# Two halves of the first layer's weights fetched and converted ahead of the first attention units

## The chip, the cores and the metric

The kernel runs on one core of one Trainium2 chip. Times are device microseconds of one execution; the time before is the median of three runs. Besides the times there is one profiled execution, whose trace all rows below come from.

## What is computed

A block of local and global attention, and behind it two feed-forward layers, all in float32. 4 batches with 8 heads, 512 local and 32 global positions of 64 values each; the attention's rows, 2176 of 512 values, go through the two layers, each 512 to 2048 to 512.

```python
s_g = scale * np.matmul(q_g, k_all.transpose(0, 1, 3, 2))
out_g = np.matmul(sm(s_g), v_all)
mask = np.abs(pos[:, None] - pos[None, :]) <= window
s_ll = np.where(mask, s_ll, -1000000000.0)
s_l = np.concatenate([s_lg, s_ll], axis=-1)
out_l = np.matmul(sm(s_l), np.concatenate([v_g, v_l], axis=2))
...
h = x @ w_in                                       # first layer
g = np.maximum(h, 0.0) + alpha * np.minimum(h, 0.0)
x = g @ w_out
h = x @ w_in2                                      # second layer
g = h * np.clip(h + 3.0, 0.0, 6.0) / 6.0
out = g @ w_out2
```

## The kernel before

**Units.** Local attention is cut into 32 units, each a batch, one of two halves of the sequence and a pair of heads. A unit loads queries and keys (`qk_t`, 368 KB, L169) and values (`v_t`, 512 KB, L180). `scores` (L187 and on) takes two units at a time: their products go to two PSUM banks, one for each head of the pair, and a bank holds both units (L194). `softmax` reads four pieces of a unit on VectorE (L212), each with a read of an accumulator, takes four exponentials on ScalarE (L216), then adds and inverts the sums (L218, L220). `transposes` turns the four pieces on TensorE (L227) and ScalarE copies them out as `pt` (L229); `values` multiplies with `v_t` (L240) and VectorE scales the result into `xo` (L246).

**First layer.** `x_from_attention` transposes `xo` (L409) and splits it into a high and a low part, `xt`: a cast on ScalarE (L395) and a subtraction on VectorE (L396). Four such splits make the first lane of 256 columns; its pieces come from units 0 to 3. The first block of rows has two lanes, the second of which (units 4 to 7) follows four steps behind. Each step makes one 128-row piece of h with 12 products (L424), an activation (L434 ScalarE, L436 VectorE, L442 ScalarE, L443 VectorE), and 12 products into y (L455).

**Weights.** The weights come as float64 numbers, which the kernel sees as pairs of 32-bit words; it loads 512 KB of them into a buffer `raw` (L94, five buffers), and `to_float32` and `split_w` turn them into float32 and then into a high and a low part of a weight tile `wt`. A tile has two halves, one for each product of the layer, and there are 32 halves. A half takes, in this order: on ScalarE the low words (L109); on VectorE a multiplication of the high words (L113) and two bit operations (L117, L119); on ScalarE the cast to the high part (L125); on VectorE the subtraction for the low part (L126). `Weights.convert(1)` emits one half. While the first units run, `CONVERT` says after which steps of the attention this is done.

**What sets the order.** The program is written in one sequence, and a scheduler moves instructions past one another on each engine, by dependencies and its own estimates. `here(...)` pins an instruction to its place in program order. Every engine then works through its own list strictly in that order, and SP issues the loads in the order of its list.

## Time and profile before

| | |
|---|---|
| median of three runs | 842.88 us (842.30 to 843.77) |
| the profiled execution | 842.45 us |
| its span | 840.4 us |
| TensorE busy (PE) | 820.3 us, 98% |
| VectorE busy (DVE) | 592.8 us, 71% |
| ScalarE busy (ACT) | 415.2 us, 49% |

The shares are those of the whole span, which has an attention stage, a first layer and a second layer with different limits. The first block of rows ends at about 152 us; the conversions of the first layer's weights lie in it. A row of the timeline gives start and duration of an instruction, or of several merged, and in brackets how long its engine had been idle before and what ended that.

### The profile page before, as it was taken

To read this page: it belongs to the slowest core of one execution; us is meant where nothing else is said; L and a number is where in the kernel's file an instruction comes from. 1 tells how busy PE (TensorE), PEld (TensorE's weight loads), DVE (VectorE), ACT (ScalarE), POOL (GpSimd) and SP (SyncE) were. 2 spreads that over 40 slices of the span, in tenths; PEclk is the share of its full clock that TensorE was granted. 3 is DMA by queue.
4 is the path that set the end of the run, shared out by engine and by line. 5 is a ranking of instruction groups with operands and counts; after the bars stand their busy time and mean duration, and the time that the engine had idled before them with its cause. 6 is when DMAs were issued, how large, how long until landed. Compare 5 with 4: busy or idle time off the path is not lost.

```text
span 840.4 us, 18272 instructions
## 1 busy us (share of the span) xinstructions
PE 820.3 (98%) x7228; PEld 741.4 (88%) x7228; DVE 592.8 (71%) x1319; ACT 415.2 (49%) x905; POOL 0.2 (0%) x4
## 2 busy tenths in 40 slices
PE   7889999999999999989999999999999999999997
PEld 5779999888888888878899988889999998999996
DVE  4989995477878786787677847768967776954221
ACT  5876665465656554465454524434543444542222
POOL 0000000000000000000000000000000000000000
PEclk9999999999999999999999999999999999999999
DMA  9976563357768876798586566657776878888882
GB/s 336 349 252 227 182 225 112 113 202 259 274 214 305 262 260 231 256 314 285 181 266 204 156 208 194 192 184 228 208 247 210 281 244 248 265 270 260 285 256 68
DMA packets 72868, 195.70 MB, mean 233 GB/s; under 512 B 7120, under 2 KB 18384, under 8 KB 72784
## 3 DMA queue, kind: packets, MB, share of 16 engines
q1 hardware_dynamic: 72688, 194.42, 70.0%
q8 instruction: 57, 0.93, 0.5%
q14 instruction: 27, 0.22, 0.1%
q10 hardware_dynamic: 96, 0.13, 0.1%
HBM read 152.05 MB, written 42.47 MB: 231 GB/s over the span
## 4 chain that ended last, share of the span: by engine, by line
PE 86%; DVE 5%; ACT 4%; DMA 3%; issue 1%; SPq 0%; ACTq 0%; DVEq 0%
PE y_ps L455 20%; PE h_ps L424 19%; PE o_ps L859 17%; PE k_ps L776 16%; PE h_ps L926 4%; PE o_ps L714 4%; ACT p L216 2%; PE s_ps L194 1%; DMA raw<-in_w 1%; PE o_ps L240 1%; PE pt_ps L227 1%; DVE z L117 1%; DVE z L119 1%; ACT raw L109 1%; PE xt_ps L409 1%
## 5 line engine op out<-in xcount | busy, mean ns | idle before, releaser
L455 PE MATMUL y_ps<-g,wt 128*128 128x256 f32 (+2 forms) x1152 | 209.1, 331 | 4.2 <-ACT wt L125 2.5
L424 PE MATMUL h_ps<-xt,wt 128*128 128x256 f32 (+2 forms) x1152 | 207.1, 330 | 1.7 <-DVE xt L396 1.2
L455 PEld LDWEIGHTS y_ps<-g,wt 128*128 128x128 f32 x1152 | 176.5, 189 | 23.4 <-ACT wt L125 3.1
L424 PEld LDWEIGHTS h_ps<-xt,wt 128*128 128x128 f32 x1152 | 178.4, 191 | 19.0 <-DVE xt L396 1.5
L859 PE MATMUL o_ps<-ws,gh 128*128 128x256 f32 x784 | 139.9, 283 | 2.0 <-DMA ws<-wo 2.0
L776 PE MATMUL k_ps<-bt,ws 128*128 128x512 f32 (+1 forms) x672 | 136.8, 362 | 0.0
L776 PEld LDWEIGHTS k_ps<-bt,ws 128*128 128x128 f32 x672 | 120.8, 188 | 12.8
L859 PEld LDWEIGHTS o_ps<-ws,gh 128*128 128x128 f32 x784 | 120.5, 192 | 2.8 <-DMA ws<-wo 2.6
L859 PE MATMUL o_ps<-ws,gl 128*128 128x256 f32 x392 | 106.6, 283 | 0.0
L789 ACT CAST gh<-far 128x1024 fp32r<-128x1024 f32 (+1 forms) x56 | 52.8, 942 | 61.7 <-PE o_ps L859 56.0
L790 DVE TENSOR_TENSOR gl<-far,gh 128x1024 fp32r<-128x1024 f32 (+1 forms) x56 | 60.8, 1088 | 30.3 <-ACT gh L789 30.1
L436 DVE SCALAR_TENSOR_TENSOR t<-t,c_sb,h_ps 128x256 f32<-128x256 f32 (+2 forms) x96 | 55.2, 587 | 32.2 <-ACT t L434 31.9
L859 PEld LDWEIGHTS o_ps<-ws,gl 128*128 128x128 f32 x392 | 73.3, 192 | 0.1
L434 ACT ACTIVATE t<-h_ps 128x512 f32<-128x512 f32 (+2 forms) x84 | 42.9, 512 | 53.4 <-PE h_ps L424 52.2
L442 ACT CAST g<-t 128x512 fp32r<-128x512 f32 (+2 forms) x84 | 45.3, 539 | 44.0 <-DVE t L436 43.9
L443 DVE TENSOR_TENSOR g<-t,g 128x512 fp32r<-128x512 f32 (+2 forms) x84 | 49.1, 586 | 21.3 <-ACT g L442 18.7
L761 ACT ACTIVATE t<-far,half_sb 128x512 f32<-128x512 f32 (+1 forms) x48 | 32.1, 670 | 51.9 <-DVE far L757 51.9
L216 ACT ACTIVATE p<-p,st 128x128 f32<-128x128 f32 x128 | 49.7, 391 | 12.2 <-DVE st L212 12.1
L109 ACT ACTIVATE raw<-raw,quarter_sb 128x512 uint32<-128x512 uint32 x64 | 49.7, 777 | 3.2 <-DMA raw<-in_w 3.2
L117 DVE SCALAR_TENSOR_TENSOR z<-z,raw 128x512 uint32<-128x512 uint32 x64 | 43.7, 689 | 3.3 <-ACT raw L109 0.8
L119 DVE SCALAR_TENSOR_TENSOR z<-raw,z 128x512 uint32<-128x512 uint32 x64 | 43.5, 686 | 0.7
L926 PE MATMUL h_ps<-xt,ws 128*128 128x384 f32 x192 | 36.0, 336 | 0.0
(100 smaller groups left out, 856.8 us busy)
## 6 DMA issues: line engine op xcount, KB each, us to landing
ws<-wo SPq DMA_DIRECT2D x72, 512.0 KB, 4.3
raw<-in_w SPq DMA_DIRECT2D x64, 512.0 KB, 5.8
ws<-wi SPq DMA_DIRECT2D x64, 512.0 KB, 4.6
v_t<-in_vE SPq DMA_DIRECT2D x32, 512.0 KB, 7.3
qk_t<-in_qkE SPq DMA_DIRECT2D x32, 368.0 KB, 5.2
wi<-raw SPq DMA_DIRECT2D x16, 512.0 KB, 3.1
wi<-parts SPq DMA_DIRECT2D x16, 512.0 KB, 4.6
wo<-raw SPq DMA_DIRECT2D x16, 512.0 KB, 4.4
```

The costliest lines, as they stand in the source:

```text
L109: here(nc.scalar.activation(low, low, AF.Relu, bias=quarter_sb, scale=0.9 * 2.0 ** -29))
L117: nc.vector.scalar_tensor_tensor(out=bits, in0=bits, scalar=3, in1=low, op0=ALU.logical_shift_left, op1=ALU.bitwise_or)
L119: nc.vector.scalar_tensor_tensor(out=bits, in0=high, scalar=0x80000000, in1=bits, op0=ALU.bitwise_and, op1=ALU.bitwise_or)
L216: nc.scalar.activation(p[:, n, :], p[:, n, :], AF.Exp, bias=st[:, 1, n:n + 1], scale=-1.0, accum_out=st[:, 2, n:n + 1])
L424: nc.tensor.matmul(ps[:, a:b], lhsT=wts[j][:, 0, wl, 128 * c:128 * c + 128], rhs=xt[c][:, xl, a:b], start=k == 0, stop=k == 3 * NC - 1)
L436: nc.vector.scalar_tensor_tensor(out=t[:, c:d], in0=t[:, c:d], scalar=c1_sb[:, j:j + 1], in1=ps[:, c:d], op0=ALU.mult, op1=ALU.add)
L455: nc.tensor.matmul(y[c][:, a:b], lhsT=wts[j][:, 1, wl, 128 * c:128 * c + 128], rhs=g[:, gl, a:b], start=first, stop=last, skip_group_check ...
L776: nc.tensor.matmul(bank, lhsT=wt[:, wl, at:at + 128], rhs=bt[x][:, c, xl, 0:w], start=first and k == 0, stop=k == 5, skip_group_check=True)
L789: nc.scalar.copy(hi, src)
L790: nc.vector.tensor_tensor(out=lo, in0=src, in1=hi.bitcast(F32), op=ALU.subtract)
L859: nc.tensor.matmul(bank, lhsT=part[:, jp, 128 * c:128 * c + 128], rhs=wo[:, jp, 256 * wl:256 * wl + 256], start=opens, stop=k == NP // 2 - ...
L926: nc.tensor.matmul(h, lhsT=wt[:, wl, 128 * c:128 * c + 128], rhs=xt[c][:, xl, 0:w], start=k == 0, stop=k == 3 * NC - 1)
```

## The change

1. SP's list: the first raw words (`raw`) are loaded ahead of the first unit's `qk_t`, the second ahead of the other three units' `qk_t`. New `yield`s in `local_units` and new calls of `W1.fetch` do this.
2. The scores of units 0 and 1 are made by two calls of `scores`, so that each unit has two banks of its own; the pairs after that stay as they are.
3. `CONVERT` becomes (1, 2, 3, 4, 5): five halves are emitted beside the first units, not three.
4. For halves 0 and 1 the low words are taken by a shift on VectorE (`LOW_ON_DVE`), not by the activation on ScalarE. For halves 0 to 3 (`FREE`) the first instructions aren't pinned.

```diff
-CONVERT = (3, 4, 5)
+LOW_ON_DVE = 2
+FREE = 4
+CONVERT = (1, 2, 3, 4, 5)
...
-        here(nc.scalar.activation(low, low, AF.Relu, bias=quarter_sb, scale=0.9 * 2.0 ** -29))
+        place = (lambda x: x) if free else here
+        if first:
+            nc.vector.tensor_scalar(out=low, in0=low, scalar1=29, scalar2=None, op0=ALU.logical_shift_right)
         else:
-            here(nc.scalar.activation(z, high.bitcast(F32), AF.Copy, scale=2.0 ** -112))
+            place(nc.scalar.activation(low, low, AF.Relu, bias=quarter_sb, scale=0.9 * 2.0 ** -29))
+        place(nc.vector.tensor_scalar(out=z, in0=high.bitcast(F32), scalar1=2.0 ** -112, scalar2=None, op0=ALU.mult))
...
-    def split_w(raw, wt, m):
-        z = to_float32(raw)
+    def split_w(raw, wt, m, k):
+        z = to_float32(raw, k < LOW_ON_DVE, k < FREE)
...
         nc.sync.dma_start(out=consts_sb, in_=consts)
+        yield
         load(1)
         load(2)
+        yield
...
-        scores(*pairs[0])
+        for u in pairs[0]:
+            scores(u)
...
-    attention_steps(1)
     W1.fetch(1)
     attention_steps(1)
     W1.fetch(2)
+    attention_steps(1)
+    attention_steps(1)
+    W1.fetch(3)
+    attention_steps(1)
+    W1.fetch(4)
```

SP's list at the start of the program, before:

```order
L169 DMA qk_t<-in_qkE 128x736
L255 DMA consts_sb<-in_consts 128x528
L169 DMA qk_t<-in_qkE 128x736 x3
L180 DMA v_t<-in_vE 128x1024 x2
L94 DMA raw<-in_w 128x512
```

and now:

```order
L96 DMA raw<-in_w 128x512
L171 DMA qk_t<-in_qkE 128x736
L257 DMA consts_sb<-in_consts 128x528
L96 DMA raw<-in_w 128x512
L171 DMA qk_t<-in_qkE 128x736 x3
L182 DMA v_t<-in_vE 128x1024 x2
L96 DMA raw<-in_w 128x512
```

Two loads of raw words moved ahead of the first units' loads, and a third stands behind the first two loads of values.

VectorE's list behind the softmax of units 0 to 3, before (`st_175`, `st_221` and `st_233` are the sums of units 1, 2 and 3, `raw_121` the first half's words):

```order
L212 ISA st_233 128x1
L218 TENSOR_SCALAR st_175<-st_175 128x4
L220 RECIPROCAL rs_185<-st_175 128x4
L218 TENSOR_SCALAR st_221<-st_221 128x4
L220 RECIPROCAL rs_231<-st_221 128x4
L218 TENSOR_SCALAR st_233<-st_233 128x4
L220 RECIPROCAL rs_243<-st_233 128x4
L269 TENSOR_SCALAR c1_sb_73<-consts_sb_72 128x16
L113 TENSOR_SCALAR z_268<-raw_121 128x512
```

and now, between unit 1 and unit 2 (`st_181` belongs to unit 1, `st_235` to unit 2, `raw_125` is the third half's words):

```order
L128 TENSOR_TENSOR wt_264<-z_265,wt_264 128x512
L220 TENSOR_SCALAR st_181<-st_181 128x4
L222 RECIPROCAL rs_191<-st_181 128x4
L118 TENSOR_SCALAR z_288<-raw_125 128x512
L214 ISA p_150,st_235<-s0_ps_201,consts_sb_72 128x128
```

Before, no conversion stands ahead of the softmax of any of the first four units. Now the first half's conversion stands ahead of unit 0, the second half's ahead of unit 1, and the third half's first instruction, which waits for its words, ahead of unit 2.

ScalarE's list from its start, before (`p` are the exponentials, four to a unit):

```order
L216 ACTIVATE p,st<-p,st 128x128 x9
L229 COPY pt<-pt_ps 128x512
L216 ACTIVATE p,st<-p,st 128x128 x5
L229 COPY pt<-pt_ps 128x512
L216 ACTIVATE p,st<-p,st 128x128 x2
L109 ACTIVATE raw<-raw,quarter_sb 128x512
L229 COPY pt<-pt_ps 128x512 x2
```

and now:

```order
L127 CAST wt<-z 128x512
L218 ACTIVATE p,st<-p,st 128x128 x4
L127 CAST wt<-z 128x512
L218 ACTIVATE p,st<-p,st 128x128 x4
L117 ACTIVATE raw<-raw,quarter_sb 128x512
L218 ACTIVATE p,st<-p,st 128x128 x4
L231 COPY pt<-pt_ps 128x512
L218 ACTIVATE p,st<-p,st 128x128 x4
L231 COPY pt<-pt_ps 128x512
L127 CAST wt<-z 128x512
L117 ACTIVATE raw<-raw,quarter_sb 128x512
L231 COPY pt<-pt_ps 128x512 x2
```

The casts of three halves and the low words of the third and fourth moved in among the first four units' exponentials and copies. Towards the end of the first block the lists of all four engines become those of before, and they stay the same to the program's end.

## Rows read from the trace of the kernel before

**Rows 1.** The page: the chain that ended last, by engine.

```profile
PE 86%; DVE 5%; ACT 4%; DMA 3%; issue 1%; SPq 0%; ACTq 0%; DVEq 0%
```

**Rows 2.** Windows: busy us of each engine, granted clock, DMA share, GB/s.

```profile
core 0: us, PE busy (x) PEld busy (x) DVE busy (x) ACT busy (x) POOL busy (x), PEclk, DMA share, GB/s
0.00:10.00 10.00, 8.17 (x138) 5.56 (x139) 2.04 (x20) 3.11 (x10) 0.20 (x4) 1.00 0.78 264
10.00:20.00 10.00, 6.94 (x148) 4.28 (x146) 7.01 (x36) 8.84 (x33) 0.00 (x0) 1.00 1.03 402
60.00:70.00 10.00, 9.42 (x82) 9.07 (x87) 8.93 (x18) 6.45 (x12) 0.00 (x0) 1.00 0.59 201
120.00:130.00 10.00, 10.00 (x191) 9.25 (x190) 9.59 (x22) 4.63 (x8) 0.00 (x0) 1.00 0.35 105
130.00:140.00 10.00, 10.00 (x86) 10.00 (x86) 4.77 (x23) 5.75 (x23) 0.00 (x0) 1.00 0.51 176
21.00:22.00 1.00, 1.00 (x30) 0.59 (x14) 1.00 (x3) 1.00 (x2) 0.00 (x0) 0.50 1.04 414
```

**Rows 3.** Timeline, first 24 us: start, duration, engine, line, instruction, idle before.

```profile
4.62 1.11 PE L194 MATMUL s_ps<-qk_t 64*32 64x128 f32 x32
...
7.84 0.29 DVE L212 CUSTOM_DVE_ANT_0 p<-s_ps,consts_sb 128x128 f32<-128x128 f32 x1 [6.93 <-PE s_ps L194]
...
8.18 0.40 ACT L216 ACTIVATE p<-p,st 128x128 f32<-128x128 f32 x1 [6.17 <-DVE st L212]
...
15.30 0.74 ACT L109 ACTIVATE raw<-raw,quarter_sb 128x512 uint32<-128x512 uint32 x1
...
20.06 0.46 PE L409 MATMUL xt_ps<-consts_sb,xo 128*128 128x128 f32 x2 [1.67 <-DVE xo L246]
...
23.33 0.42 DVE L396 TENSOR_TENSOR xt<-xt_ps,xt 128x256 fp32r<-128x256 f32 x1
```

**Rows 4.** Groups by line and form, 0 to 152 us: busy us, mean ns, idle.

```profile
L216 ACT ACTIVATE p<-p,st 128x128 f32<-128x128 f32 x72 | 28.0, 391 | 7.1 <-DVE st L212 7.1
L109 ACT ACTIVATE raw<-raw,quarter_sb 128x512 uint32<-128x512 uint32 x32 | 25.0, 782 | 3.2 <-DMA raw<-in_w 3.2
L117 DVE SCALAR_TENSOR_TENSOR z<-z,raw 128x512 uint32<-128x512 uint32 x32 | 21.6, 688 | 0.7
L119 DVE SCALAR_TENSOR_TENSOR z<-raw,z 128x512 uint32<-128x512 uint32 x32 | 21.5, 684 | 0.1
L126 DVE TENSOR_TENSOR wt<-z,wt 128x512 fp32r<-128x512 f32 x32 | 21.5, 686 | 2.8 <-ACT wt L125 2.4
L125 ACT CAST wt<-z 128x512 fp32r<-128x512 f32 x32 | 19.3, 616 | 12.0 <-DVE z L119 11.7
...
L113 DVE TENSOR_SCALAR z<-raw 128x512 f32<-128x512 f32 x32 | 13.4, 422 | 0.0
...
L229 ACT COPY pt<-pt_ps 128x512 f32<-128x512 f32 x16 | 8.6, 578 | 1.1 <-PE pt_ps L227 1.1
```

**Rows 5.** Loads issued at 0.7, 1.1, 1.6 and 5.7 us: KB, us to landing.

```profile
qk_t<-in_qkE SPq DMA_DIRECT2D x1, 368.0 KB, 3.1
...
consts_sb<-in_consts SPq DMA_DIRECT2D x1, 264.0 KB, 3.3
...
qk_t<-in_qkE SPq DMA_DIRECT2D x1, 368.0 KB, 5.0
...
v_t<-in_vE SPq DMA_DIRECT2D x1, 512.0 KB, 10.2
```

**Rows 6.** Timeline of PE: products of h while the granted clock is low.

```profile
40.68 2.56 PE L424 MATMUL h_ps<-xt,wt 128*128 128x256 f32 x11
```

**Rows 7.** Timeline of PE: the second lane's first products, and two waits.

```profile
49.66 3.14 PE L424 MATMUL h_ps<-xt,wt 128*128 128x256 f32 x24 [1.22 <-DVE xt L396]
53.99 0.74 PE L455 MATMUL y_ps<-g,wt 128*128 128x256 f32 x4 [1.19 <-ACT wt L125]
...
60.58 3.39 PE L455 MATMUL y_ps<-g,wt 128*128 128x256 f32 x24 [1.09 <-ACT wt L125]
```

More of the change, by code (lines that the diff above doesn't have):

```diff
@@ L99, in fused_kernel, with to_float32 @@
     here = tc.keep_in_program_order
-    def to_float32(raw, on_dve=True):
+    def to_float32(raw, first=False, free=False):
         words = raw.bitcast(U32).rearrange("p (f two) -> p f two", two=2)
         low, high = words[:, :, 0], words[:, :, 1]
-        here(nc.scalar.activation(low, low, AF.Relu, bias=quarter_sb, scale=0.9 * 2.0 ** -29))
         z = work.tile([128, 512], F32, tag="z", name="z", bufs=ZB)
         bits = z.bitcast(U32)
-        if on_dve:
-            here(nc.vector.tensor_scalar(out=z, in0=high.bitcast(F32), scalar1=2.0 ** -112, scalar2=None,
-                                         op0=ALU.mult))
-        else:
-            here(nc.scalar.activation(z, high.bitcast(F32), AF.Copy, scale=2.0 ** -112))
+        place = (lambda x: x) if free else here
+        if first:
+            nc.vector.tensor_scalar(out=low, in0=low, scalar1=29, scalar2=None, op0=ALU.logical_shift_right)
+        else:
+            place(nc.scalar.activation(low, low, AF.Relu, bias=quarter_sb, scale=0.9 * 2.0 ** -29))
+        place(nc.vector.tensor_scalar(out=z, in0=high.bitcast(F32), scalar1=2.0 ** -112, scalar2=None, op0=ALU.mult))
         nc.vector.scalar_tensor_tensor(out=bits, in0=bits, scalar=3, in1=low, op0=ALU.logical_shift_left,
@@ L155, in convert @@
                     self.wt[j] = wp.tile([128, 2, 2, 512], F32R, tag="w", name="wt", bufs=NJ)
-                split_w(self.raw.pop(k), self.wt[j], m)
+                split_w(self.raw.pop(k), self.wt[j], m, k)
                 self.fetch(k + EARLY + 1)
```

## The prediction

> **What bounds the kernel now.** I read the chain that ended last first. It lies on TensorE for 86% of the span [rows 1], so a change that adds or removes no product can only pay where TensorE has holes. The busy times by stretches of ten microseconds, read next, say where these are [rows 2]: TensorE is busy for 8.17 and 6.94 of the first two tens, 9.42 from 60 to 70, and 10.00 from 120 on. VectorE is the other way round: 2.04 and 7.01 busy in the first two tens, then about nine in ten until 130 us, where it drops to 4.77 because the 32 conversions of the first layer are over. So from about 20 to 110 us VectorE sets the pace with conversions, TensorE follows with little slack, and behind that TensorE alone counts. Since all lists are the same again from the end of the first block on, whatever time TensorE has gained or lost there goes to the end one to one. All that matters is the first 110 us.
>
> The start itself is read from the timeline [rows 3]. The first scores begin at 4.62 us. VectorE idles 6.93 us until 7.84, because the bank that holds unit 0 also takes unit 1. ScalarE's exponentials run from 8.18 on, the first low words at 15.30, the last split of the first lane's `xt` at 23.33 to 23.75. A half costs VectorE 0.422 + 0.688 + 0.684 + 0.686 = 2.48 us and ScalarE 0.782 + 0.616 = 1.40 us [rows 4].
>
> **Part 1, the credit: conversions done earlier.** I count VectorE's list up to the last split of the first lane. Before, it holds 3 L113, 3 L117, 2 L119 and 2 L126; now 5, 5, 5 and 4 of them. The surplus is 2 x 0.422 + 2 x 0.688 + 3 x 0.684 + 2 x 0.686 = 5.64 us [rows 4] that VectorE need not do later. The two shifts in place of ScalarE's low words are new and aren't credit: their nearest row is L113, one operand and the same stride, 0.42 us; the upper bound is a bit operation, 0.69 us; the lower bound is no less than L113, since nothing on VectorE that reads 512 words is cheaper in these rows. I take 0.42 each, 0.84 us, with at most 0.54 more. They lie in VectorE's idle start. Taking 2 x 0.78 = 1.56 us from ScalarE is in the walk below.
>
> **Part 2, the debit: the first lane comes later.** Loads land in the order of issue. By their landings [rows 5] the first `qk_t` (0.377 MB) is there at 0.73 + 3.1 = 3.8 us, the constants (0.647 MB in all) at 1.17 + 3.3 = 4.5, the second `qk_t` (1.02 MB) at 1.64 + 5.0 = 6.6, the fourth `v_t` (4.40 MB) at 5.7 + 10.2 = 15.9. I read the new list against this curve of bytes. The first words, 0.52 MB, land at 4.2; the first `qk_t`, now 0.90 MB, at 5.9 (before 3.8); the constants, 1.17 MB, at 7.0; the second words, 1.70 MB, at 8.2; and the third words, which are now the ones that make up 4.40 MB, at 15.9.
>
> The walk, VectorE and ScalarE in the order of their lists with the durations of [rows 4]. Half 0: shift and three steps, 4.2 to 6.4. Softmax of unit 0 at 7.1, when the constants are there (before 7.84); its exponentials end at 9.0. Half 1, words at 8.2, behind half 0's subtraction: done at 11.0. Only now comes unit 1 on VectorE, and on ScalarE the cast of half 1 comes ahead of its exponentials: 11.7 to 13.3, and VectorE's sums of unit 1 to 13.65. Then both engines stand before the third half's words, VectorE with L113 and ScalarE with L109, until 15.9: 2.3 us of VectorE and 2.6 us of ScalarE, with the softmax of units 2 and 3 queued behind them and, behind that, TensorE's transposes. From 15.9 ScalarE has low words 0.78, eight exponentials 3.13, two copies 1.16, a cast 0.62, low words 0.78, two copies 1.16: 7.6 us, to 23.5. `xo` of units 2 and 3 needs the last copy and their products with the values, and VectorE still has two splits in front: done at 26.0. Then L113 0.42, a subtraction 0.69, L117 0.69, a split 0.42, L119 0.68, the last split 0.42: 29.3 us. Before it ended at 23.75. The debit is 5.55 us.
>
> Its lower end: at the 402 GB/s of 10 to 20 us [rows 2], 4.40 MB take 10.9 us, and with the 2.2 us that the first load needs beyond its own 0.9 us (3.1 - 0.9) the third words land at 13.1, before VectorE asks for them; the stand of 2.3 to 2.8 us is gone and the debit is 2.75 us. Its upper end is the clock, below.
>
> **Part 3, small terms.** TensorE's list has 48 products of y ahead of the second lane instead of 36. The dozen is worth 12 x 3.14/24 = 1.6 us [rows 7] if TensorE is the bound behind it, nothing while VectorE is; between 60 and 70 us they are busy for 9.42 and 8.93 of ten [rows 2], so I take half, -0.8, and the bounds 0 and -1.6. The separate banks let unit 0's softmax go ahead without unit 1's scores; that is in the walk, and the constants at 7.0 leave 0.7 us of it. What of that is hidden: unit 1's softmax then waits for half 1 anyway.
>
> The clock. Between 21 and 22 us TensorE's granted clock is 0.50, the 1.2 GHz level [rows 2]; TensorE had idled 1.67 us just before 20.06 [rows 3]. In the walk it idles from about 13.6 to 18.4 us, so the slow level is likely for the first lane. 11 products at that level took 2.56 us, 0.233 each, against 0.131 at the full one [rows 6, 7]. Of the 24 products of the first two pieces, 9 wait for the splits anyway; 15 x 0.102 = 1.5 us is the most, none the least. VectorE covers about 1 us of it with the fifth half's subtraction and bit operation; I take +0.5. The Trainium skill, "TensorE: Matmul & The Clock Gate", section "HAM oscillation — how this bites in real kernels", says of this that idle gaps put the array back to half rate and that it should be kept fed, which speaks against emptying TensorE here; by that rule the full +1.5 would stand in the sum in place of +0.5. The trace agrees as far as the row at 21 us goes.
>
> **Sum.** -5.64 + 5.55 - 0.8 + 0.5 = -0.4 us against the profiled execution, which took 842.45 us (span 840.4 and 2.05 around it). It lies 0.43 below the median of the three runs, 842.88, so for a median I add that: 842.5 us. Own range of this case: -2.8 (words earlier) to +1.8 (products worth nothing, clock full), 839.7 to 844.3.
>
> **Rivals.**
> A, faster: the third words land before they are asked for. For it: the rate of 402 GB/s is reached at 10 us; against it: the curve of bytes is a measured one and has the slow stretch in it. Then the first lane ends at 26.5, VectorE's credit isn't eaten, and the kernel takes 842.5 - 2.8 = 839.7 us. It decides at 13.65 us.
> B, slower: the late first lane isn't paid back. If TensorE and not VectorE is the true bound from the second lane on, credit counts only as far as TensorE waited on weights, 1.19 + 1.09 us [rows 7]; the rest of the conversions done earlier only makes VectorE idle later. Then +5.55 - 2.3 + 0.5 = +3.75, 846.6 us. For it: TensorE is busy 9.42 of ten from 60 us on. Against it: VectorE at 8.93 with waits of ScalarE's on it. It decides by the start of the second lane, now 49.66 [rows 7]. By then VectorE's list has 9 whole halves against 8 before, so only 5.64 - 2.48 = 3.16 us of the credit can have been used, and I expect it at 49.66 + 5.55 - 3.16 = 52 us; beyond 53 us B holds.
> C, the clock: TensorE stays at 1.2 GHz through the first lane and what follows it; +1.5 for +0.5, 843.5 us.
> D, it doesn't do what it says: the first words don't land ahead of the first `qk_t`, the idle start stays empty and half 0 comes as late as unit 0's sums; one half, 2.5 us, of the credit is lost: 845.0 us.
>
> **Chances.** Forecast 0.40, A 0.30, B 0.20, C 0.06, D 0.04. A measurement of this kernel tells 0.2%, 1.7 us, from no change, so the same is 841.2 to 844.6. A and a little of the forecast are faster: 0.33; B, D and a little of the forecast are slower: 0.26; same 0.41. The range takes in A and most of B, with the shift's 0.54: 839.3 to 846.3.
>
> **What would show it.** In the trace after: the shift of half 0 starting near 4.2 us; the first exponential near 7.5; VectorE and ScalarE idle until the third words near 15.9 (A: no such wait); the last split of the first lane near 29 us (A: 26.5); the second lane's 24 products near 52 us (B: beyond 53); the 1.09 us wait of TensorE for weights gone; granted clock 0.5 somewhere between 18 and 30 us; VectorE's busy share falling a few us earlier than 130. The forecast is wrong if scheduling between 30 and 110 us, where the four lists differ in many small places that I didn't price one by one, moves more than these 3 us.

## The result: slower by 0.9%

The changed kernel takes 850.32 us (median of four, 849.46 to 852.19) against 842.59 for the kernel before (four, 841.2 to 843.77): a ratio of 1.0093, 95% interval 1.0068 to 1.0117. The profiled execution took 849.91 us, its span 848.1. The forecast was 842.5 with a range to 846.3; it was wrong.

Line numbers of the changed kernel are a little higher: L115 is the new shift of the low words on VectorE, L117 the low words on ScalarE (L109 before), L118, L119 and L121 the three steps of a conversion (L113, L117, L119), L127 and L128 cast and subtraction (L125, L126), L401 the split of `xt` (L396), L429 the products h (L424), L460 the products y (L455).

**The whole.** The chain of the changed kernel, share of the span by engine, against [rows 1]:

```profile
PE 91%; DMA 4%; ACT 2%; DVE 2%; issue 0%; SPq 0%; ACTq 0%; DVEq 0%
```

Windows of the changed kernel, columns as in [rows 2]: busy us of PE, PEld, DVE, ACT, POOL, then granted clock, DMA share, GB/s.

```profile
0.00:10.00 10.00, 5.50 (x64) 3.77 (x72) 4.63 (x20) 3.51 (x10) 0.20 (x4) 1.00 0.76 273
10.00:20.00 10.00, 6.62 (x132) 4.42 (x113) 6.63 (x35) 5.97 (x25) 0.00 (x0) 0.85 1.03 409
20.00:30.00 10.00, 8.90 (x140) 6.43 (x134) 7.64 (x18) 5.45 (x14) 0.00 (x0) 0.50 1.03 404
30.00:40.00 10.00, 9.29 (x109) 7.73 (x108) 6.15 (x29) 6.90 (x25) 0.00 (x0) 0.96 0.47 163
60.00:70.00 10.00, 6.49 (x53) 6.09 (x51) 5.83 (x11) 6.05 (x11) 0.00 (x0) 1.00 0.38 143
```

Two things stand out against [rows 2]. VectorE is busier in the first ten (4.63 for 2.04), as meant, but from 30 to 40 it is busy for only 6.15. And from 60 to 70 both TensorE and VectorE have a hole (6.49 and 5.83, before 9.42 and 8.93).

**The start went as walked.** Timeline of the changed kernel, first 31 us (start, duration, engine, line, in brackets the engine's idle time before and what ended it), against [rows 3]:

```profile
5.15 0.43 DVE L115 TENSOR_SCALAR raw<-raw 128x512 uint32<-128x512 uint32 x1 [4.23 <-DMA raw<-in_w]
...
16.19 0.43 DVE L118 TENSOR_SCALAR z<-raw 128x512 f32<-128x512 f32 x1 [2.27 <-DMA raw<-in_w]
16.19 0.76 ACT L117 ACTIVATE raw<-raw,quarter_sb 128x512 uint32<-128x512 uint32 x1 [2.69 <-DMA raw<-in_w]
...
30.22 0.37 ACT L400 CAST xt<-xt_ps 128x256 fp32r<-128x256 f32 x1 [2.52 <-PE xt_ps L414]
...
30.62 0.43 DVE L401 TENSOR_TENSOR xt<-xt_ps,xt 128x256 fp32r<-128x256 f32 x1 [1.28 <-ACT xt L400]
```

The shift starts at 5.15 (walked: 4.2), both engines stand before the third half's words until 16.19 (walked: 15.9; waits 2.27 and 2.69, walked 2.3 and 2.6), and the last split of the first lane ends at 31.05 (walked: 29.3; before 23.75).

**The second lane and what follows it.** Timeline of the changed kernel, PE and ACT, from the second lane's first products to the end of the first block, against [rows 7]:

```profile
56.51 3.10 PE L429 MATMUL h_ps<-xt,wt 128*128 128x256 f32 x24
...
64.44 0.74 ACT L117 ACTIVATE raw<-raw,quarter_sb 128x512 uint32<-128x512 uint32 x1 [2.22 <-DMA raw<-in_w]
65.09 0.60 ACT L447 CAST g<-t 128x512 fp32r<-128x512 f32 x1
...
65.75 3.13 PE L460 MATMUL y_ps<-g,wt 128*128 128x256 f32 x24 [2.39 <-ACT g L447]
...
70.26 0.38 PE L429 MATMUL h_ps<-xt,wt 128*128 128x256 f32 x1 [1.38 <-ACT wt L127]
...
70.99 4.50 PE L429 MATMUL h_ps<-xt,wt 128*128 128x256 f32 x23 [0.34 <-DVE wt L128]
...
159.57 5.63 PE L429 MATMUL h_ps<-xt,wt 128*128 128x512 f32 x24
```

The second lane starts at 56.51 (before 49.66, forecast 52). Then TensorE waits 2.39, 1.38 and 0.34 us for ScalarE and VectorE (before 1.19 and 1.09 us), and the 23 products after that take 4.50 us, 0.196 each, where 0.131 is the full rate [rows 7]: the granted clock is 0.50 from 72 to 75. The second block's first products, 512 columns wide, begin at 159.57. In the kernel before they begin here:

```profile
151.97 4.27 PE L424 MATMUL h_ps<-xt,wt 128*128 128x512 f32 x18
```

That is 7.60 us later, and it goes to the end one to one: 849.91 - 159.57 = 690.3 us remain, before 842.45 - 151.97 = 690.5.

So the loss can be cut at three points: the first lane's last split (+7.30), from there to the second lane's first products (25.46 for 25.91: -0.45), and from there to the end of the first block (103.06 for 102.31: +0.75). Windows of the kernel before, then of the changed one, cut at these points:

```profile
23.75:49.66 25.91, 22.54 (x375) 18.91 (x374) 23.80 (x95) 21.58 (x74) 0.00 (x0) 0.93 0.85 299
49.66:151.97 102.31, 99.73 (x1244) 95.76 (x1245) 87.53 (x236) 65.10 (x159) 0.00 (x0) 1.00 0.59 202
```

```profile
31.05:56.51 25.46, 23.90 (x410) 19.39 (x409) 21.28 (x90) 20.88 (x75) 0.00 (x0) 1.00 0.66 220
56.51:159.57 103.06, 98.95 (x1235) 95.47 (x1233) 85.68 (x232) 63.94 (x155) 0.00 (x0) 0.98 0.57 192
```

Between the lanes VectorE is idle for 4.18 of the 25.46 us, TensorE for only 1.56: it has twelve more products of y there and 28 more of the scores, and is busy for 23.90. That points away from VectorE as what sets the pace; no_sign below tests it. Behind the second lane TensorE idles 4.11 us for 2.58.

Where did VectorE's head start go? The third step of a conversion (L119 before, L121 now), counted by stretches: the column with x is VectorE's. Before:

```profile
0.00:10.00 10.00, 0.00 (x0) 1.00 0.78 264
10.00:20.00 10.00, 0.68 (x1) 1.00 1.03 402
20.00:30.00 10.00, 2.06 (x3) 0.83 1.03 404
30.00:40.00 10.00, 1.37 (x2) 1.00 0.87 299
```

After:

```profile
0.00:10.00 10.00, 0.69 (x1) 1.00 0.76 273
10.00:20.00 10.00, 1.38 (x2) 0.85 1.03 409
20.00:30.00 10.00, 1.37 (x2) 0.50 1.03 404
30.00:40.00 10.00, 0.00 (x0) 0.96 0.47 163
```

By 20 us three halves are done against one, by 30 five against four, by 40 five against six: the lead is gone. The sixth half's words had landed at 23.5, but in the lists of ScalarE and VectorE it stands behind the first lane's activations, because the program asks for conversions step by step (`AHEAD`), and its low words (L117) run only at 38.30.

### The profile page after: what moved, and what is told of

The parts are those of the page before. It is cut to its first block, busy times and chain, and to the rows that moved or that the text cites. A ratio compares the mean times of both kernels' runs of the same rounds, so it can differ in the third digit from the quotient of the medians.

```text
span 848.1 us, 18269 instructions
## 1 busy us (share of the span) xinstructions
PE 824.1 (97%) x7228; PEld 744.5 (88%) x7228; DVE 595.2 (70%) x1321; ACT 414.2 (49%) x903; POOL 0.2 (0%) x4
## 4 chain that ended last, share of the span: by engine, by line
PE 91%; DMA 4%; ACT 2%; DVE 2%; issue 0%; SPq 0%; ACTq 0%; DVEq 0%
PE y_ps L460 22%; PE h_ps L429 21%; PE o_ps L864 17%; PE k_ps L781 15%; PE h_ps L931 4%; PE o_ps L719 4%; DMA raw<-in_w 2%; PE s_ps L196 2%; PE o_ps L242 2%; PE pt_ps L229 1%; PE xt_ps L414 1%; DMA ws<-wo 1%; ACT p L218 1%; PE gs_ps L337 1%; PE go_ps L382 1%; DMA qk_t<-in_qkE 1%
## 5 line engine op out<-in xcount | busy, mean ns | idle before, releaser
L460 PE MATMUL y_ps<-g,wt 128*128 128x256 f32 (+2 forms) x1152 | 209.1, 331 | 4.7 <-ACT g L447 4.6
L429 PE MATMUL h_ps<-xt,wt 128*128 128x256 f32 (+2 forms) x1152 | 208.5, 331 | 2.1 <-ACT wt L127 1.4
L460 PEld LDWEIGHTS y_ps<-g,wt 128*128 128x128 f32 x1152 | 176.5, 189 | 23.8 <-ACT g L447 5.2
L429 PEld LDWEIGHTS h_ps<-xt,wt 128*128 128x128 f32 x1152 | 179.6, 192 | 19.4 <-ACT wt L127 1.6
L441 DVE SCALAR_TENSOR_TENSOR t<-t,c_sb,h_ps 128x256 f32<-128x256 f32 (+2 forms) x96 | 55.2, 588 | 35.7 <-ACT t L439 35.4
L117 ACT ACTIVATE raw<-raw,quarter_sb 128x512 uint32<-128x512 uint32 x62 | 47.9, 772 | 6.7 <-DMA raw<-in_w 6.7
L119 DVE SCALAR_TENSOR_TENSOR z<-z,raw 128x512 uint32<-128x512 uint32 x64 | 43.9, 690 | 3.1 <-ACT raw L117 0.8
L121 DVE SCALAR_TENSOR_TENSOR z<-raw,z 128x512 uint32<-128x512 uint32 x64 | 43.7, 688 | 0.9
```

The lines of the kernel that those rows point to most:

```text
L117: place(nc.scalar.activation(low, low, AF.Relu, bias=quarter_sb, scale=0.9 * 2.0 ** -29))
L429: nc.tensor.matmul(ps[:, a:b], lhsT=wts[j][:, 0, wl, 128 * c:128 * c + 128], rhs=xt[c][:, xl, a:b], start=k == 0, stop=k == 3 * NC - 1)
L441: nc.vector.scalar_tensor_tensor(out=t[:, c:d], in0=t[:, c:d], scalar=c1_sb[:, j:j + 1], in1=ps[:, c:d], op0=ALU.mult, op1=ALU.add)
L460: nc.tensor.matmul(y[c][:, a:b], lhsT=wts[j][:, 1, wl, 128 * c:128 * c + 128], rhs=g[:, gl, a:b], start=first, stop=last, skip_group_check ...
```

## The experiments

Each time is a median of its runs; ratios are to runs of the kernel before on the same chip, with 95% intervals. "First lane" is the end of its fourth split of `xt`; "between" goes from there to the second lane's first products; "behind" from there to the first 512-wide products; "done" is the number of halves whose third step has ended when the second lane starts. These four come from one profiled execution each, which lies up to 4 us from the median.

| kernel | us | ratio | first lane | between | behind | done |
|---|---|---|---|---|---|---|
| before | 842.59 | | 23.75 | 25.9 | 102.3 | 8 |
| changed | 850.32 | 1.0093 [1.0068, 1.0117] | 31.05 | 25.5 | 103.1 | 9 |
| banks_only | 843.75 | 1.0016 [1.0002, 1.0030] | 24.9 | 26.7 | 102.4 | 9 |
| loads_only | 849.09 | 1.0075 [1.0048, 1.0103] | 26.7 | 28.8 | 102.0 | 8 |
| two_early | 844.19 | 1.0017 [1.0000, 1.0034] | 24.9 | 27.3 | 100.2 | 9 |
| ahead_3 | 845.85 | 1.0038 [1.0017, 1.0059] | 28.8 | 28.9 | 97.6 | 10 |
| v_apart | 849.02 | 1.0083 [1.0059, 1.0107] | 30.4 | 26.2 | 103.6 | 9 |
| two_early_v_apart | 844.64 | 1.0029 [1.0010, 1.0048] | 25.0 | 27.1 | 100.1 | 9 |
| third_sooner | 847.29 | 1.0065 [1.0044, 1.0086] | 30.1 | 26.6 | 101.9 | 10 |
| before_v_apart | 842.29 | 1.0002 [0.9984, 1.0020] | 23.9 | 25.4 | 101.9 | 8 |
| q5_apart | 848.12 | 1.0073 [1.0044, 1.0102] | 28.8 | 25.1 | 103.5 | 9 |
| v_buffers | 850.89 | 1.0102 [1.0056, 1.0148] | 28.9 | 29.4 | 99.4 | 10 |
| before_v_buffers | 845.04 | 1.0035 [1.0025, 1.0045] | 23.6 | 32.5 | 99.4 | 10 |
| two_early_v_buffers | 851.08 | 1.0093 [1.0064, 1.0122] | 24.9 | 37.4 | 100.2 | 10 |
| no_sign | 845.90 | 1.0041 [1.0020, 1.0062] | 31.2 | 26.9 | 100.2 | |
| two_early_ahead_3 | 846.35 | 1.0050 [1.0029, 1.0070] | 24.9 | 33.0 | 98.0 | 10 |
| before_ahead_3 | 844.59 | 1.0026 [1.0015, 1.0038] | 24.2 | 32.4 | 96.8 | 10 |
| one_early | 847.49 | 1.0059 [1.0036, 1.0081] | 24.7 | 28.8 | 105.8 | 8 |
| one_early_one_bank | 847.93 | 1.0065 [1.0047, 1.0083] | 26.4 | 30.8 | 99.7 | 10 |
| one_early_sooner | 845.12 | 1.0024 [1.0006, 1.0042] | 23.4 | 31.9 | 101.6 | 9 |

### Which part of the change costs

**banks_only**, the kernel before with

```
-        scores(*pairs[0])
+        for u in pairs[0]:
+            scores(u)
```

> The kernel before with one edit: units 0 and 1 take banks of their own. If the early conversions and loads made the change slow, this stays within 1.7 us of the kernel before (841 to 844): the first softmax starts about 2 us earlier than 7.84, but the first raw words still land at 13.5. If the two additional banks are to blame (later tiles wait for a bank), it is slower by 3 us or more, with TensorE or ScalarE waiting in the first 25 us.

Measured 843.75, 0.16% above the kernel before: nearly nothing, as expected, though the lists behind it change and the first lane comes 1.1 us later. The banks explain at most a small part of the loss.

**loads_only**, the changed kernel with

```
-LOW_ON_DVE = 2
-FREE = 4
-CONVERT = (1, 2, 3, 4, 5)
+LOW_ON_DVE = 0
+FREE = 0
+CONVERT = (3, 4, 5)
...
-        for u in pairs[0]:
-            scores(u)
+        scores(*pairs[0])
```

> The changed kernel with its loads in the new order, but the conversions where the kernel before has them (three halves, behind the values of units 0 and 1), pinned, low words on ScalarE, and units 0 and 1 in common banks. If the order of loads costs, the first softmax comes about 1 to 2 us later than 7.84 and the first lane's last split later than 23.75: 843 to 846. If the loss needs the early conversions, 841 to 844.

Measured 849.09: 7 us slower than before, more than either theory gave, without one conversion in the idle start. The new order of loads, with the lists that the scheduler makes of it, costs nearly as much as the whole change. Its first lane is 3.0 us late (the first softmax begins at 10.67 for 7.84, when unit 1's scores in the common banks are done), and the stretch between the lanes is 2.9 us longer. Timeline of loads_only, the second lane's first products:

```profile
55.53 3.02 PE L428 MATMUL h_ps<-xt,wt 128*128 128x256 f32 x23 [1.08 <-DVE xt L400]
```

**two_early**, the changed kernel with

```
-FREE = 4
-CONVERT = (1, 2, 3, 4, 5)
+FREE = 2
+CONVERT = (1, 2, 5)
```

so that two halves are still converted early, and the third half's first instructions stand behind the products with the values of units 2 and 3 instead of ahead of their softmax.

> The changed kernel with two halves converted early instead of five (CONVERT (1, 2, 5), FREE 2): the third half's first instructions stand behind the products of units 2 and 3. Theory 1 (the third raw words, at 16 us, hold up units 2 and 3 on VectorE and ScalarE, and that makes the first lane late): last split of the first lane at 22 to 25 us instead of 31.05, second lane before 51 us instead of 56.51, in all 839 to 844. Theory 2 (the first lane's delay is not the cause; loads of raw words come late between 57 and 70 us): the first lane is early but the stall stays, 847 to 850.

Measured 844.19, 6 us faster than the change. Timeline of two_early, last split of the first lane, second lane:

```profile
24.47 0.42 DVE L401 TENSOR_TENSOR xt<-xt_ps,xt 128x256 fp32r<-128x256 f32 x1
...
52.24 2.30 PE L429 MATMUL h_ps<-xt,wt 128*128 128x256 f32 x17 [0.84 <-DVE xt L401]
```

Theory 1 holds for the first lane (24.89, expected 22 to 25); the second lane comes a little later than "before 51". With the same first loads as the change, it is the third to fifth halves standing ahead of the first lane that made most of the delay; some of the 6 us may be the clock's, which is full from 20 to 30 us in this profile and 0.50 in that of the changed kernel. Two halves in the idle start still don't gain on the kernel before: 1.0017, interval 1.0000 to 1.0034.

**third_sooner**, the changed kernel with the third half's words loaded one step of the attention earlier:

```
     W1.fetch(2)
     attention_steps(1)
-    attention_steps(1)
     W1.fetch(3)
     attention_steps(1)
+    attention_steps(1)
     W1.fetch(4)
```

> The changed kernel with the third half's raw words loaded ahead of the fourth qk_t and the first v_t. Theory 1 (VectorE and ScalarE stand 2.3 and 2.7 us before the third words, which delays the first lane): the words land near 11 instead of 16.2, no such wait, the first lane's last split at 27 to 29 instead of 31.05. Under theory 1 alone the whole time falls by 2 to 4 us, 846 to 848; if the second lane hangs on the loads of v_t behind the eleventh raw load (theory 4), it falls only as far as these come sooner.

Measured 847.29. The words land at 11.5 and the waits of 2.27 and 2.69 us are gone, but the first lane only moves from 31.0 to 30.1: the whole third half now runs from about 12 to 16.3, in the place of the wait, and the softmax of unit 2 still begins at 16.2. Not the wait as such delays units 2 and 3 but anything of the third half ahead of them.

### The clock in the first lane, and what comes with a late first lane

**v_apart** and **before_v_apart**, the changed kernel and the kernel before with

```
-            nc.sync.dma_start(out=v_t[u], in_=vE[b, hp, :, 8 * hf:8 * hf + 8])
+            (nc.gpsimd if u in (6, 7) else nc.sync).dma_start(out=v_t[u], in_=vE[b, hp, :, 8 * hf:8 * hf + 8])
```

> The changed kernel with two loads on another queue: v_t of units 6 and 7 is issued by GpSimd instead of SyncE; the lists of VectorE and ScalarE stay as they are. Theory 4 (in the change SyncE issues these two loads at 44.05 behind a raw load that waits for a free buffer until the sixth half is converted at 41.2; they land at 51.6, 8.3 us later than before, and the second lane waits for them): they land before 42, the second lane starts at 50 to 53 us instead of 56.51, in all 844 to 847. If the second lane is late for another reason (conversions, the late first lane, the clock), the second lane stays beyond 55 and the time at 849 to 851.

> The kernel before with v_t of units 6 and 7 on GpSimd's queue. There SyncE issues them at 34.93, behind the tenth raw load, which waits for a buffer until 33.2; they land at 43.3 and the second lane starts at 49.66. Theory 4: the second lane starts 1 to 4 us earlier, 839.5 to 842. If a load issued by GpSimd is itself slow or the second lane hangs on VectorE's conversions, 842 to 844.

Theory 4 fell. Measured 849.02 and 842.29. On GpSimd's queue the two loads are issued no sooner; timeline of v_apart:

```profile
43.41 1.19 POOL L182 DMA_DIRECT2D v_t<-in_vE  x2 [42.97 <-PE o_ps L242]
```

They wait for their two buffers, which the values of units 4 and 5 (L242, 42.42 to 43.5) still read. SyncE's queue is not what held them. What they wait for does count: in v_apart the values of units 4 and 5 come 0.9 us sooner than in the changed kernel (42.42 for 43.34), but TensorE then stands before the values of unit 7 until their load has landed,

```profile
53.35 0.65 PE L242 MATMUL o_ps<-v_t,pt 128*32 128x64 f32 x32 [1.24 <-DMA v_t<-in_vE]
```

and the second lane starts at 56.53, where it starts in the changed kernel too (56.51). **two_early_v_apart**, the same edit on two_early:

> The kernel of two_early with the same two loads on GpSimd's queue. There they land at 46.4 and the second lane starts at 52.2. Theory 4 says 1 to 3 us off, 841 to 843.5. If TensorE alone sets the pace there, 844 stays.

844.64: nothing won there either, although the loads are issued 1.7 us sooner (37.73 for 39.44). The values of units 6 and 7 start at 47.27 for 47.39.

**q5_apart**, the same kind of edit for `qk_t` of unit 5 (`nc.gpsimd if u in (5,)`):

> The changed kernel with one load on another queue: qk_t of unit 5 is issued by GpSimd; the lists of VectorE and ScalarE stay as they are. In the change it is issued at 18.8 and lands at 28.2 (before 11.5 and 21.6), behind three more raw loads. Theory 5 (units 4 and 5 are late because this load is): it lands before 24, the scores of unit 5 end before 31 instead of 34.2, the second lane starts at 52 to 54 instead of 56.51, in all 845 to 848. Theory 1 (TensorE's list puts these scores behind the first lane's products, which wait for the last split at 31.05): the scores of unit 5 still end near 34, the time stays at 848 to 851.

Measured 848.12, intervals overlapping with the change's. The load lands at 17.7 instead of 28.2, but the scores of unit 5 hardly come sooner relative to the first lane. Timeline of PE in the changed kernel, then in q5_apart: the first lane's products and, behind them in TensorE's list, the scores of unit 5:

```profile
31.47 2.17 PE L429 MATMUL h_ps<-xt,wt 128*128 128x256 f32 x16
33.58 0.67 PE L196 MATMUL s_ps<-qk_t 64*32 64x128 f32 x32
```

```profile
28.87 2.18 PE L429 MATMUL h_ps<-xt,wt 128*128 128x256 f32 x16
30.98 0.67 PE L196 MATMUL s_ps<-qk_t 64*32 64x128 f32 x32
```

Theory 5 fell, theory 1 holds: the scores stand behind the first lane's products, which wait for the last split, and in the changed kernel too the load had landed (28.2) five us before they began. The numbers alone would have spoken for theory 5 (the second lane at 53.91, expected 52 to 54; the scores' end at 31.65, expected before 31), so here the outcome misleads: what moved the first lane and the scores by 2.2 to 2.6 us is something else. Windows of q5_apart:

```profile
10.00:20.00 10.00, 6.51 (x124) 4.25 (x108) 6.35 (x35) 5.63 (x23) 0.66 (x1) 0.50 1.03 408
20.00:30.00 10.00, 8.49 (x177) 6.22 (x167) 8.41 (x21) 6.70 (x18) 0.00 (x0) 0.91 1.02 404
```

The granted clock is low from 10 to 20 here and nearly full from 20 to 30; in the changed kernel it is 0.85 and then 0.50, and falls between 16 and 18, when TensorE has been idle since 14.0. The lists of TensorE, VectorE and ScalarE are the same. Of what TensorE has ahead of the last transposes, the scores of unit 4 show it, in the changed kernel and then in q5_apart:

```profile
28.50 1.07 PE L196 MATMUL s_ps<-qk_t 64*32 64x128 f32 x20
```

```profile
26.82 0.63 PE L196 MATMUL s_ps<-qk_t 64*32 64x128 f32 x20
```

With the slow stretch before the transposes and products of the first lane, the last split ends at 28.84 instead of 31.05, the second lane starts at 53.91 instead of 56.51, the block ends at 157.37 instead of 159.57, and the span is 845.7 instead of 848.1. v_apart, again with the same lists, has 0.67 and 0.58 there and its first lane between the two, at 30.4; what it won by that was lost at the wait for the load of unit 7. So from q5_apart to the changed kernel the late first lane is passed on one to one, and where the slow stretch falls is worth about 2.2 us, by one profile of each.

### What the conversions done early are worth

**ahead_3**, the changed kernel with `AHEAD = 3` for 2.

> The changed kernel with the conversions asked for one step further ahead (AHEAD 3 instead of 2): the sixth half is converted ahead of the first lane's activations and from there on two halves more are always done. Theory 3 (the two halves that were converted early are given back at once, because the list asks for the next ones only step by step, and VectorE idles between 31 and 40 us): VectorE's busy time from 30 to 40 us rises from 6.15 towards 9, the second lane starts 2 to 4 us earlier than 56.51, in all 844 to 848. If TensorE alone bounds after the late first lane, the same as the change, 849 to 851; if raw words are short, slower than the change.

Measured 845.85. The idle time from 30 to 40 is filled (VectorE 8.74 of ten), but the second lane does not come sooner, as theory 3 said it would: it starts later. Timeline of ahead_3, the second lane's first products:

```profile
57.67 6.00 PE L429 MATMUL h_ps<-xt,wt 128*128 128x256 f32 x48
```

The gain lies behind it, 97.6 us for 103.1, with TensorE idle for 0.4 us there instead of 4.1. That the time lies within theory 3's 844 to 848 is luck.

**no_sign** leaves out the third step of the conversion (the sign bit, L121) for the sixth to eleventh halves, 6 x 0.69 = 4.1 us of VectorE's work, most of it between the lanes:

```
-        nc.vector.scalar_tensor_tensor(out=bits, in0=high, scalar=0x80000000, in1=bits, op0=ALU.bitwise_and,
-                                       op1=ALU.bitwise_or)
+        if sign:
+            nc.vector.scalar_tensor_tensor(out=bits, in0=high, scalar=0x80000000, in1=bits, op0=ALU.bitwise_and,
+                                           op1=ALU.bitwise_or)
...
-        z = to_float32(raw, k < LOW_ON_DVE, k < FREE)
+        z = to_float32(raw, k < LOW_ON_DVE, k < FREE, not 5 <= k < 11)
```

> The changed kernel without the third step of the conversion (the sign bit, 0.69 us of VectorE) for the sixth to eleventh halves, those that are converted between the first lane and the second: 4.1 us of VectorE less there. Part of the computation is left out. Forecast's view (VectorE sets the pace up to the second lane): the stretch between the last splits of the two lanes falls from 27.1 to 23 to 25 us, the whole to 845 to 847. Theory 6 (the attention of units 4 to 7 sets it, through TensorE's order, ScalarE and loads): the stretch stays at 26 to 28 us; the whole 848 to 850 or a little less, where raw buffers come free earlier.

The stretch between the lanes does not shrink: its window, columns as above, has VectorE busy for 19.96 us of 26.92.

```profile
31.19:58.11 26.92, 25.14 (x410) 20.76 (x410) 19.96 (x91) 20.70 (x73) 0.00 (x0) 0.93 0.68 223
```

From last split to last split, as the expectation counts it, it takes 28.2 us for 27.1. The granted clock is lower here (0.93 for 1.00): the sixteen products of the first lane that take 2.17 us in the changed kernel (31.47) take 3.45, as this line shows.

```profile
32.13 3.45 PE L430 MATMUL h_ps<-xt,wt 128*128 128x256 f32 x16
```

Without these 1.3 us the stretch would be about as long as in the changed kernel, and not 4 us shorter. So in these profiles VectorE does not set the pace there (theory 6). The whole is nevertheless 4.4 us faster than the change by the medians: 845.90, within what the forecast's view expected and below theory 6's 848 to 850. The profiled execution, 849.5, is the longest of its seven (843.27 to 849.5), so where a usual execution saves these 4 us is not shown. In the profile the stretch behind the second lane is shorter, 100.2 for 103.1; its lists differ there in the order that the next section is about.

**before_ahead_3** and **two_early_ahead_3**, the same `AHEAD = 3` on the kernel before and on two_early:

> The kernel before with the conversions asked for one step further ahead, nothing else. First lane unchanged near 23.7; the conversions then stand ahead of the attention of units 4 to 7, so the second lane comes 1 to 3 us later than 51.9, and the first block behind it is 2 to 4 us shorter than 100.0. In all 840 to 843.5. If TensorE alone bounds it, 842 to 844.

> The kernel of two_early with the conversions asked for one step further ahead. two_early has its first lane at 24.9, 29.0 us to the second lane's last split, 98.6 to the end of the first block; ahead_3 has 28.8, 31.0 and 95.5. If the parts add up (first lane from two_early, the rest between the two): 24.9 + 29 to 31 + 95.5 to 98, so the block ends at 149.5 to 154 (before 152.0) and the whole takes 840 to 844. If the second lane comes later by all that the conversions take ahead of it, 844 to 846.

Measured 844.59 and 846.35, each some 2 us slower than without. Behind the second lane both are shorter (96.8 and 98.0 for 102.3 and 100.2), but the second lane starts 7 and 6 us later: the conversions stand ahead of the attention of units 4 to 7. The parts did not add up as hoped for two_early_ahead_3: its second lane's last split comes 35.7 us behind the first lane's, and not 29 to 31.

**v_buffers**, **before_v_buffers**, **two_early_v_buffers**: buffers of their own for `v_t` of units 4 to 7,

```
-            if u < FIRST_UNITS:
+            if u < 2 * FIRST_UNITS:
                 if u % 2 == 0:
```

> The changed kernel with buffers of their own for v_t of units 4 to 7, so that units 6 and 7 need not wait for the values of units 4 and 5 (43.3 to 44.4) and then 8 us for the load. Theory 4b (this chain through two buffers carries the delay of units 4 and 5 into the second lane): v_t of unit 7 lands before 40 instead of 51.6, the values of units 6 and 7 start at 49 to 51 instead of 52.4, the second lane 1.5 to 3 us earlier than 56.51, in all 846 to 849. If the scores and exponentials of units 6 and 7 are as late as their values, nothing is won: 849 to 851.

> The kernel before with the same buffers. There the values of units 6 and 7 start at 44.9, 1.2 us behind the last transposes (43.7) and 1.6 behind the landing of v_t of unit 7 (43.3). So at most 1 us is to be won: 841 to 842.5; if the second lane hangs on VectorE's conversions, 842 to 843.

> The kernel of two_early (two halves early, the third behind units 2 and 3) with the same buffers. There v_t of unit 7 lands at 46.4, the transposes end at 45.8, the values start at 47.4 and the second lane at 52.2. Theory 4b: values at 46, second lane at 50.5 to 51.5, in all 842 to 843.5. If TensorE's order sets it: 844.

All three miss: 850.89, 845.04 and 851.08. The edit did not do what it was meant to: with the new buffers the loads of `v_t` for units 8 and 9 move ahead in SyncE's list, and those of units 6 and 7 are issued later, at 49.34, 42.94 and 49.20 (changed kernel 44.05, before 34.93, two_early 39.44). TensorE then waits for them: 4.10 us in before_v_buffers, 3.19 in two_early_v_buffers. Lines of v_buffers, the two loads and the values of unit 7:

```profile
49.34 0.90 SPq L182 DMA_DIRECT2D v_t<-in_vE  x2
...
56.31 0.65 PE L242 MATMUL o_ps<-v_t,pt 128*32 128x64 f32 x32 [0.45 <-DMA v_t<-in_vE]
```

So theory 4b, that the chain through the two buffers carries the delay into the second lane, was not tested by these runs. The stretch between the lanes is 29.4 to 37.4 us in them.

**one_early**, **one_early_one_bank**, **one_early_sooner**: one half alone is converted early, its words loaded behind the first `qk_t` and the constants (one_early_sooner: ahead of the constants).

```
-LOW_ON_DVE = 2
-FREE = 4
-CONVERT = (1, 2, 3, 4, 5)
+LOW_ON_DVE = 1
+FREE = 1
+CONVERT = (1, 4, 5)
...
         load(1)
         load(2)
-        yield
         load(3)
...
-    W1.fetch(1)
     attention_steps(1)
+    W1.fetch(1)
+    attention_steps(1)
     W1.fetch(2)
-    attention_steps(1)
     attention_steps(1)
     W1.fetch(3)
-    attention_steps(1)
-    W1.fetch(4)
```

In one_early_one_bank, `scores(*pairs[0])` stands again in place of the loop; in one_early_sooner, the first `yield` stands ahead of the constants' load.

> The changed kernel with one half converted early (CONVERT (1, 4, 5), LOW_ON_DVE 1, FREE 1), its raw words loaded behind the first qk_t and the constants; the second half's words behind v_t of unit 1 as in the kernel before. If a half converted in VectorE's idle start is a half less ahead of the first lane's last split: the first lane at 21.5 to 23.5 instead of 23.75, in all 840.5 to 842. If the loads that it pushes back (second to fourth qk_t, 0.52 MB or 1.3 us) eat it: 842 to 844.

> As one_early, with units 0 and 1 in common banks as in the kernel before. The softmax of unit 0 then waits for unit 1's scores, near 8.5, so half 0 is done wholly ahead of it. By banks_only the separate banks gain nothing: within 1.5 us of one_early.

> As one_early, with the words ahead of the constants: half 0 is done 1 us sooner and the first softmax 1 us later than in one_early. Within 1 us of one_early if the start of the softmax counts no more than the conversion; slower by 1 to 2 us if the softmax sets the first lane.

Measured 847.49, 847.93 and 845.12: all slower than before. The 0.52 MB in front push the second to fourth `qk_t` and the values back by 1 to 2.4 us, and the first lane ends at 24.7, 26.4 and 23.4 for 23.75. A half fewer to convert brings it forward by 0.3 us at best.

### A place behind the second lane

Why does the changed kernel take 103.1 us behind the second lane with nine halves done, where the kernel before takes 102.3 with eight? ScalarE's list shows it: its rows around the wait that ends at 64.44, with numbers of the buffers (raw_724, 753, 905 and 947 are loaded in this order, as twelfth to fifteenth).

```
65 L117 ACTIVATE raw_947<-raw_947,quarter_sb_87 128x512
66 L447 CAST g_933<-t_932 128x512
67 L117 ACTIVATE raw_724<-raw_724,quarter_sb_87 128x512
68 L439 ACTIVATE t_1003<-h_ps_978 128x512
69 L447 CAST g_1004<-t_1003 128x512
70 L117 ACTIVATE raw_905<-raw_905,quarter_sb_87 128x512
```

ScalarE wants the words that are loaded fifteenth (issued 57.49, landed 64.36) ahead of those loaded twelfth to fourteenth (landed 52.85, 55.13 and 61.82), and ahead of the cast of g that TensorE's products of y wait for. In the kernel before the same words stand behind that cast and behind the twelfth's.

What this costs in the changed kernel can be read from its trace. The value `t` that the cast reads is done on VectorE at 62.1; ScalarE, idle from 62.2, waits for the words until 64.44; the cast starts at 65.09 and TensorE's products behind it at 65.75.

```profile
61.26 0.87 DVE L441 SCALAR_TENSOR_TENSOR t<-t,c_sb,h_ps 128x256 f32<-128x256 f32 x2 [0.79 <-ACT t L439]
```

q5_apart and v_apart, with the same lists, have the same hole: ScalarE waits 2.39 and 3.13 us for the words and TensorE 2.56 and 3.29 us for that cast. Lines of q5_apart, then of v_apart:

```profile
63.28 4.40 PE L460 MATMUL y_ps<-g,wt 128*128 128x256 f32 x24 [2.56 <-ACT g L447]
```

```profile
66.68 5.49 PE L460 MATMUL y_ps<-g,wt 128*128 128x256 f32 x24 [3.29 <-ACT g L447]
```

In all three the low clock follows the hole (0.83 in q5_apart and 0.79 in v_apart from 60 to 70 us). These 24 products take 3.13 us in the changed kernel, where the clock falls only for the next products, by 23 x (0.196 - 0.131) = 1.5 us.

The kernels of the table fall into two groups by this place. With eight, nine and ten halves done, those with the words ahead of the cast have behind the second lane 105.8 (one_early); 103.1, 103.6, 103.5, 102.4, 101.6 (changed, v_apart, q5_apart, banks_only, one_early_sooner); 101.9 (third_sooner). Those with them behind the cast, at the same `AHEAD`, have 102.3, 101.9, 102.0 (before, before_v_apart, loads_only); 100.2, 100.1 (two_early, two_early_v_apart); 99.4, 99.4, 100.2, 99.7 (the three with buffers, one_early_one_bank). Within a group a ninth half done goes with some 2 to 4 us less behind the second lane, a tenth with at most 1.7; between the groups lie 1.4 to 3.9 us. That is read across kernels whose lists differ in other places too. And the place alone is not the price: in banks_only and one_early_sooner, which belong to the slower group, ScalarE does not wait for these words. No run moved that row alone, so what the order costs in the whole time is not shown.

## Why the prediction was wrong

By its own steps, with the profiled executions:

| step | expected | found |
|---|---|---|
| first lane's last split, with the clock | +5.55 + 0.5 | +7.30 |
| from there to the second lane's first products | -3.16 | -0.45 |
| from there to the end of the first block | -2.48 - 0.8 | +0.75 |
| the rest | 0 | -0.14 |
| sum | -0.4 | +7.46 |

**The walk (debit) was right up to 20 us; the clock was put too small.** Order, waits and landings of the first 20 us came within 1 us of the walk. In q5_apart, with the slow clock ahead of the first lane's last steps, the last split ends at 28.84 (walked 29.3). In the profile of the changed kernel the low clock lies on 20 to 30 us instead and costs 2.2 us more. I had given the clock 0.5, from the products of h alone, and left out the rest of TensorE's list ahead of the last transposes: the products with the values of the last unit (1.08 us for 0.65 in q5_apart), the scores of unit 4 (1.07 for 0.63) and the transposes themselves. ScalarE waits 2.52 us for these before 30.22, a wait that the walk does not have. By the rule of the Trainium skill, "TensorE: Matmul & The Clock Gate", section "HAM oscillation — how this bites in real kernels", that idle gaps put the array back to half rate, the full 1.5 us would have stood in the sum. The 2.2 us found between the two profiles go further in that direction.

**VectorE as the pacemaker up to the second lane was wrong.** That is the step that failed first: of the 3.16 us booked there 0.45 were found. It was read from VectorE's busy share of nine tenths [rows 2]. But TensorE was busy nearly as long there, in the changed kernel for all but 1.56 of 25.46 us, and the second lane needs the attention of units 4 to 7: scores, softmax, exponentials, transposes, values, `xo`, `xt`. The scores of unit 5 stand in TensorE's list behind the first lane's products, so they start late when these do. Over the changed kernel, v_apart and q5_apart, with the same lists of TensorE, VectorE and ScalarE, the stretch is 25.1 to 26.2 us whatever the first lane's time; taking 4.1 us of work from VectorE there (no_sign) did not shorten it in the profile. Which link of the attention sets the pace instead, TensorE's own list or the load of the values through two buffers, is open: TensorE waits 1.24 us for that load in v_apart and has no such wait in the changed kernel. Besides, the dozen products of y that I booked as -0.8 behind the second lane were paid ahead of it.

**The credit behind the second lane was real but was taken back.** The count came out as forecast, nine halves done for eight, and across the kernels a ninth half goes with 2 to 4 us less there. But the sum had -3.28 for this stretch and +0.75 was found, a miss of 4.03 us and the largest of the three. TensorE's waits for weights, which the forecast expected to shrink, grew: where ScalarE's list stands before the words loaded fifteenth, ahead of the cast of g, TensorE is idle for 2.39 us, then for 1.38 and 0.34, and then has 1.5 us of low clock. That makes 5.6 us, against 1.19 + 1.09 before [rows 7]. The prediction named scheduling between 30 and 110 us as what it had not priced; by the trace most of the miss lies there.

**The rivals.** B had the right condition (second lane beyond 53 us) and the right sign: the late first lane was not paid back. Its price, +3.75, took the debit as 5.55 instead of 7.3 and let 2.3 us of TensorE's waits for weights vanish; they grew instead (2.58 us idle behind the second lane before, 4.11 after). A's condition failed: the words were waited for until 16.19. D failed: the first half was converted from 5.15 on. C had the clock, but at +1.5, where the two profiles lie 2.2 apart.

**What no run settles.** loads_only lost 7 us by the order of loads alone, and two_early, with that order and two halves early, only 2; the scheduler writes other lists for each, so the shares of loads and conversions in the 7.7 us don't add up. The order of words at ScalarE was not changed by itself, the chain of `v_t` through two buffers was not shortened by any run, and none of the versions was faster than the kernel before.

## What to carry to other kernels

An engine that is busy for nine tenths need not be the pacemaker: book work taken from it as credit only where a wait of the engine behind it names it, and look at what else gates the next stage. Before work is put into an idle start, look whether its loads or its first waiting instruction stand in a list ahead of the chain that starts everything; here a delay of 7.3 us there was not made up later (7.5 at the end), and no version gained by the idle start. After an edit, look in the new lists whether it did what it was meant to: buffers of their own made two loads later, not sooner. And compare the order in which an engine asks for loads with the order in which they are issued, near each stage's start.

## What the runs showed of the hardware

Where TensorE's low clock falls is not fixed by the lists of the engines that compute. In three kernels with the same lists of TensorE, VectorE and ScalarE (two loads or one are issued from another queue), the granted clock was 0.85 and 0.50 in the stretches 10 to 20 and 20 to 30 us of one profile, 0.67 and 0.58 in another, 0.50 and 0.91 in a third, and the span 848.1, 849.3 and 845.7. The second has besides a wait of 1.24 us for a load. Over the runs of one kernel the time goes with the mean granted clock of the whole span, though not strictly: no_sign's seven runs go from 849.5 us at 0.986 to 843.27 at 0.994, ahead_3's ten from 849.67 at 0.985 to 843.86 at 0.992, with one of 841.57 at 0.990. So the clock is probably part of why runs of one kernel lie up to 8 us apart, and one profile of each kernel can't price a term of 2 us.
